# An earlier start for the first three tiles, in a kernel with an S5 scan and a gated MLP on one core

## The chip, the cores and the metric

The kernel runs on one core of one Trainium2 chip. The metric is the device time of one execution in microseconds (us). Profiles show the engines of the core: PE (matmul) and PEld (its weight loads), DVE, ACT, POOL, and SPq, the queue from which the DMAs are issued. A profile's span is 1.8 to 2.1 us shorter than the time of the same execution (261.9 us in a run of 263.81 us). The granted clock is the share of PE's full clock that the profile records (1.0 is all of it; it reads 1.00 even up to 4.4 us in the kernel before, where the warm matmuls come only every 0.43 us, so it does not show the slow start). The record calls two kernels the same when their times differ by less than 2%; all the differences below but one (e6, unclear) are of that class, and are read from ratios with their intervals, and from the traces.

## The reference, cut to what matters

```python
x = A_x                                   # 2048 x 640, bf16
xn = _layernorm(x)
z  = gelu(xn @ w_in)                      # 640 x 1728: z1 is the first half, z2 the second
z2 = _layernorm(z[..., 864:])
g  = w_sp @ z2 + b_sp                     # 2048 x 2048
mlp = (z[..., :864] * g) @ w_out
Bu = xn @ B_bar^T                         # complex; h_t = Lam_bar * h_(t-1) + Bu_t
out = x + (2 * Re(h @ C^T) + xn * Dskip) + mlp
```

## The kernel before: the parts that matter

The program is written as a list of operations with the memory that each reads and writes. A scheduler in the kernel simulates them with estimated durations and gives each engine a fixed order. PE's order is the program's; the orders of DVE, ACT and the DMA queue come out of that simulation. On the chip every engine keeps its order, whatever comes early or late.

```python
DMA_BW = 280e3                            # the simulation's DMA rate, bytes per us
...
FIRST = "x0 x1 x2 h002 h025 x3 h105 x4 x5"  # first loads: tiles of x, parts of w_in (half, from k, to k)
...
def ln_x(i):                              # statistics: bn_stats on DVE, or two sums on ACT for some tiles
    ...                                   # rstd = (var + 1e-5) ** -0.5 on POOL
    dve(... tensor_scalar(xn, x, mean, rstd, subtract, mult) ...)     # L545
def xn_T(i):                              # tiles 0-5: five PE transposes and a copy from PSUM
    if i in DMA_T:                        # tiles 6-15: one DMA transpose in SBUF      L369
...
def bu(q, tq):                            # B u: real and imaginary rows together, two PSUM banks
    for k in range(ND):
        for ri in range(2):
            r = e.matmul(ps[:, b + ri, :], btv[:, ri, k, q*128:(q+1)*128], xnTv[:, k, tq*512:(tq+1)*512], ...)
...
xn_T(0, 0); xn_T(1, 1)                    # PE's order for the first tiles
z2_half(0, 0, 2); z2_half(1, 0, 3)        # five products (k = 0..4) of one tile and one half of the z2 columns
xn_T(2, 0); z2_half(0, 1, 6); xn_T(3, 1); ...
```

After the first products (z2 of 16 tiles) PE does B u, z1, the products with w_sp ("spatial" below, 448 matmuls of 432 columns) and the output products.

Of the kernel before, what the change touches and what calls it, by code (L numbers as in the profile page):

```python
# [28 lines left out]
class _Graph:  # L29
# [6 lines left out]
    DMA_BW = 280e3  # L36
    DMA_BW_T = 215e3

    def __init__(self):
# [46 lines left out]
    def schedule(self):  # L86
# [32 lines left out]
        while left:  # L119
            best = None  # L120
            for eng, lst in avail.items():
                if not lst:
                    continue
                f = free.get(eng, 0.0)
                if eng == "pe":
                    if pei >= len(pe) or pe[pei].npred:
                        continue
                    cand = pe[pei]
                    st = max(f, cand.rdy)
                else:  # L130
                    s0 = min(max(f, o.rdy) for o in lst)
                    cand = max((o for o in lst if max(f, o.rdy) <= s0 + (self.EPS0 if s0 < self.TEPS else eps)), key=lambda o: o.tail)
                    st = max(f, cand.rdy)
                if best is None or st < best[0]:
                    best = (st, cand)
            st, op = best
            eng = op.eng
            avail[eng].remove(op)
            if eng == "pe":
                pei += 1  # L140
            op.start = st
            free[eng] = st + op.occ
            if op.nbytes:
                if op.lat > 2.2:
                    dma_free = max(st + 0.3, dma_free) + op.nbytes / self.DMA_BW_T
                    free[eng] = max(free[eng], dma_free)
                    op.done = max(st + op.occ, dma_free) + 1.7
                else:
                    dma_free = max(st + op.occ + 0.9, dma_free) + op.nbytes / self.DMA_BW
                    op.done = dma_free + op.lat - 0.9  # L150
            else:
                op.done = st + op.occ + op.lat
            order.setdefault(eng, []).append(op)
            left -= 1
            for s in op.succs:
                s.npred -= 1
                at = op.start + op.occ if eng == "pe" == s.eng else op.done
                if at > s.rdy:
                    s.rdy = at
                if s.npred == 0:  # L160
                    avail.setdefault(s.eng, []).append(s)
# [41 lines left out]
D = 640  # L203
ND = 5
# [8 lines left out]
def bass_parallel_sum__ssm_conv_s5__mixer_gmlp__prompt_kernel(  # L213
# [17 lines left out]
    with _cl.ExitStack() as _stack, nc.Block() as block:  # L231
# [106 lines left out]
        def bank(b):  # L338
            return ("ps%d" % b, 0, 1)
# [82 lines left out]

        def load_x(i, q="sp", bias=0.0):
            m = x_m[i]
            xs[i] = m
            dma(q, m.ap(D), A_x[0, i * 128:(i + 1) * 128, :], [], [m.iv()], 128 * D * 2,
                "x%d" % i, bias=bias)
# [28 lines left out]

        FIRST = "x0 x1 x2 h002 h025 x3 h105 x4 x5"
        for n, w in enumerate(FIRST.split()):
# [7 lines left out]
        for i in range(6, 11):  # L466
            load_x(i, bias=4500 - 10 * i)
        dma("sp", dk_m.ap(D), A_Dskip[:].partition_broadcast(128), [], [dk_m.iv()], 128 * 1280, "dskip")
        dma("sp", bsb_m.ap(16).rearrange("p (h j) -> p h j", h=2),
            B_b_sp.rearrange("(h r j) -> r h j", h=2, j=8), [], [bsb_m.iv()], 4096, "bsp")  # L470


        pool(lambda e: e.memset(zero_m.ap(512), 0.0), [], [zero_m.iv(0, 1024)], 0.5, "zero")
        pool(lambda e: e.memset(ident_m.ap(128), 0.0), [], [ident_m.iv()], 0.25, "id0")
# [8 lines left out]
            [zero_m.iv(1024, 16)], 1.4, "gelu table", bias=9000)  # L483
        NW = 11
        for n in range(NW):
# [18 lines left out]

        ACT_LN = (2, 5, 8, 11)
        ACT_Z2 = (8, 12)
        NHALF = 4
        BT_AT, BT_DEP = 10, 12
        LASTN = 480
        DMA_T = tuple(range(6, 16))  # L510
        xns = {}

        def ln_x(i):
# [4 lines left out]
            if i in ACT_LN:  # L518
# [5 lines left out]
                dve(lambda e: e.tensor_scalar(mean, stv[:, i, 0:1], 1.0 / D, None, op0=ALU.mult),  # L524
                    [siv(i, 0, 1)] + ([xns[1].iv()] if i == 2 else []), [mi], 0.07, "lnm%d" % i)
                dve(lambda e: e.tensor_tensor(stv[:, i, 2:3], mean, mean, ALU.mult),
# [4 lines left out]
            else:  # L531

                held = [xns[max(1, i - 2)].iv()] if 2 <= i < 4 else []
                dve(lambda e: e.bn_stats(stv[:, i, 0:6], x[:, 0:320]), [xm.iv()] + held, [siv(i, 0, 6)], 0.41, "bn%da" % i)
# [13 lines left out]
        def xn_T(i, b=None):  # L548
            xn = xns[i]
            if i in DMA_T:  # L550
# [8 lines left out]
            def tr(e):  # L559
                for u in range(ND):  # L560
                    r = e.transpose((v2 if i == 0 and u > 2 else v)[:, u, :], xn.ap(D)[:, u * 128:(u + 1) * 128], ident_m.ap(128))
                return r
            pe(tr, [xn.iv(), ident_m.iv()], [bank(b)] + ([bank(6)] if i == 0 else []), 0.3, "T%d" % i)
            if i == 0:
# [3 lines left out]
                    [xnT_m.iv(k * S * 2, 256) for k in (3, 4)], 0.21, "xnT0b")  # L568
            elif i % 2 == 0 or i == 1:
                act(lambda e: e.copy(xnTv[:, :, i * 128:(i + 1) * 128], v), [bank(b)], xnT_iv(i, i + 1),  # L570
                    ca(D, psum=True), "xnT%d" % i)
            else:
                dve(lambda e: e.tensor_copy(xnTv[:, :, i * 128:(i + 1) * 128], v), [bank(b)], xnT_iv(i, i + 1),
                    0.41, "xnT%d" % i)
# [16 lines left out]

        def z_mm(lhs, hcol, reads, name):
            b = pair()
            for k in range(ND):
                def mm(e, k=k):
                    for h in range(2):
# [6 lines left out]

        def z2_tile(i):
            b = z_mm(lambda k: xnTv[:, k, i * 128:(i + 1) * 128], 1, xnT_iv(i, i + 1), "z2_%d" % i)
            z = z2v[:, i, :]
# [6 lines left out]

        def z2_half(i, h, b):

            c = FH + h * FG
            for k in range(ND):
                pe(lambda e, k=k: e.matmul(ps[:, b, 0:FG], xnTv[:, k, i * 128:(i + 1) * 128], winv[:, k, c:c + FG],
                                           start=(k == 0), stop=(k == ND - 1)),
                   [xnT_m.iv((k * S + i * 128) * 2, 256), win_m.iv((k * 2 * FH + c) * 2, FG * 2)], [bank(b)], 0.1825, "z2_%d%d.%d" % (i, h, k))  # L620
            z = z2v[:, i, h * FG:(h + 1) * FG]
            s_ = 7 if h else 0
            act(lambda e: e.activation(z, ps[:, b, 0:FG], ACT.Gelu_apprx_tanh, accum_out=st2v[:, s_, i:i + 1]),
                [bank(b)], [z2iv(i, h), s2iv(s_, i, i + 1)], ca(FG, psum=True, acc=1), "gelu2_%d%d" % (i, h))
            if h:
# [48 lines left out]

        def bu(q, tq):

            b = pair()

            def mm(e):
                for k in range(ND):  # L680
                    for ri in range(2):
                        r = e.matmul(ps[:, b + ri, :], btv[:, ri, k, q * 128:(q + 1) * 128],  # L682
                                     xnTv[:, k, tq * 512:(tq + 1) * 512], start=(k == 0), stop=(k == ND - 1))
                return r
            pe(mm, xnT_iv(tq * 4, tq * 4 + 4) + [bt_m.iv()], [bank(b), bank(b + 1)], 2.16, "bu%d%d" % (q, tq))
            o = l_m.ap(4096, BF16, q * 8192).rearrange("p (j r t m) -> p r t j m", j=8, r=2, t=4)
            for ri in range(2):
                act(lambda e, ri=ri: e.copy(o[:, ri, tq], ps[:, b + ri, :].rearrange("p (m j) -> p j m", j=8)),  # L688
                    [bank(b + ri)], [l_m.iv((q * 8 + j) * 1024 + ri * 512 + tq * 128, 128) for j in range(8)],
                    ca(512, psum=True), "u%d%d%d" % (q, tq, ri))  # L690

# [533 lines left out]

        for i in range(5):
            ln_x(i)
        xn_T(0, 0)
        xn_T(1, 1)
        z2_half(0, 0, 2)  # L1230
        z2_half(1, 0, 3)
        xn_T(2, 0)
        z2_half(0, 1, 6)
        xn_T(3, 1)
        z2_half(1, 1, 7)
        z2_half(2, 0, 4)
        z2_half(2, 1, 5)
        xn_T(4, 0)
        z2_half(3, 0, 2)
        z2_half(3, 1, 3)  # L1240
        for i in range(4):
            load_x(i + 11)
        ln_x(5)
        xn_T(5, 1)
        ln_x(6)
        pslot[0] = 2
        for i in range(4, NT):
            if i + 3 < NT:
                ln_x(i + 3)
            z2_tile(i)  # L1250
            if i + 2 < NT:
                xn_T(i + 2)
            if i == BT_AT:
                load_bt(0, [xns[BT_DEP].iv()])
                load_bt(1, [xns[BT_DEP].iv()])
            if i == 4:
                s5_consts()
                load_x(15)
            if i == 6:
# [12 lines left out]
        for q in range(5):  # L1272
            for tq in range(4):
                bu(q, tq)
            if q < 4:
# [132 lines left out]
```

## Time and profile before

| | before |
|---|---|
| time, median | 263.57 us (263.48 to 264.02, 3 runs) |
| span of the profile | 261.9 us |
| busy share | PE 98%, DVE 93%, ACT 68% |
| first transposes of x on PE | 6.00 us |
| last z2 product ends, B u starts | 38.51, 38.80 us |

The timeline of PE of the kernel before, cut to the start (columns: start us, length us, engine, line, operation, out<-in, shapes, count, and in brackets PE's idle time before it and what ended it):

```profile
1.31 4.12 PE L486 MATMUL ps<-arena 128*128 128x512 bf16 x11 [1.31 <-POOL arena L480]
6.00 0.99 PE L561 MATMUL ps<-arena 128*128 128x128 bf16 x10 [0.57 <-DVE arena L545]
...
9.62 0.45 PE L561 MATMUL ps<-arena 128*128 128x128 bf16 x5 [0.60 <-DVE arena L545]
...
16.23 1.99 PE L597 MATMUL ps<-arena 128*128 128x432 bf16 x10
18.15 0.18 PE L800 MATMUL ps<-arena 15*128 15x15 bf16 x1
18.26 20.25 PE L597 MATMUL ps<-arena 128*128 128x432 bf16 x110
38.80 13.54 PE L682 MATMUL ps<-arena 128*128 128x512 bf16 x61 [0.29 <-DMA arena<-in_A_B_im_dram]
```

The row at 18.26 is tiles 5 to 15 without a hole, 0.184 us a matmul.

```profile
14.90 1.30 SPq L369 DMA_TRANSPOSE arena<-arena  x1
```

The DMA view of just that issue; its last number is the time in us from issue to landing:

```profile
arena<-arena SPq DMA_TRANSPOSE x1, 5.0
```

So tile 6 lands at 14.90 + 5.0 = 19.9 us, 0.2 us before PE wants it. The 1.30 us of the queue's row is not that time: it is only how long the queue was busy with the issue.

### The profile page before, as it was taken

Reading aid. Unit: us, or ns where it says so; the run is one execution under the profiler, and the core shown is the slowest. Engines: PE = TensorE matmul, PEld = TensorE weight load, DVE = VectorE, ACT = ScalarE, POOL = GpSimd, SP = SyncE. Lnnn points to the kernel's source line nnn. Section 1 sums busy time; section 2 is a strip of 40 time slices with the busy share of each in tenths; the row PEclk is TensorE's granted clock in tenths of the full one; section 3 lists DMA queues with packets and bytes.
Section 4 is the critical chain, followed back from the end, with each engine's and each line's share of the span. In section 5 each row is a group of like instructions: output and inputs, shape, how many; then the busy total and the mean of one; then the engine's idle time right before and its main releaser. Section 6 shows DMA issues by size and latency. Waiting matters only on the chain.

```text
span 261.9 us, 4305 instructions
## 1 busy us (share of the span) xinstructions
PE 255.5 (98%) x1487; PEld 151.6 (58%) x1491; DVE 242.3 (93%) x579; ACT 179.1 (68%) x323; POOL 23.0 (9%) x38
## 2 busy tenths in 40 slices
PE   6999999999999999999999999999999999999995
PEld 2555544444446777755555555555557777777773
DVE  4899997999899999999999999999999999999832
ACT  4899999989986545442333676976799889881110
POOL 4255084200000000000000000000000000000000
PEclk9999999999999999999999999999999999999999
DMA  6976899996001855496997858959562566447611
GB/s 185 361 100 131 178 198 227 293 242 123 0 0 38 222 154 163 121 274 125 270 212 161 210 123 197 172 86 270 154 209 45 136 171 154 98 130 205 169 51 50
DMA packets 88243, 41.97 MB, mean 160 GB/s; under 512 B 70975, under 2 KB 88223, under 8 KB 88223
## 3 DMA queue, kind: packets, MB, share of 16 engines
q1 hardware_dynamic: 88078, 41.66, 65.8%
q8 instruction: 11, 0.18, 0.3%
q14 instruction: 10, 0.07, 0.1%
q10 hardware_dynamic: 144, 0.05, 0.1%
HBM read 12.27 MB, written 12.45 MB: 94 GB/s over the span
## 4 chain that ended last, share of the span: by engine, by line
PE 64%; DVE 18%; ACT 7%; DMA 6%; issue 3%; SPq 1%; POOL 1%; DVEq 0%
PE ps L1146 22%; PE ps L682 16%; PE ps L999 12%; PE ps L597 11%; DVE arena L956 3%; DMA arena<-in_A_B_im_dram 2%; DMA g_scratch<-arena 2%; ACT arena L789 2%; DVE arena L734 2%; DVE arena L1039 2%; PE ps L1153 2%; DMA arena<-in_A_x_dram 2%; DVE arena L579 1%; DVE arena L921 1%; DVE arena L919 1%
## 5 line engine op out<-in xcount | busy, mean ns | idle before, releaser
L999 PE MATMUL ps<-arena 128*128 128x432 bf16 x448 | 82.1, 346 | 0.0
L999 PEld LDWEIGHTS ps<-arena 128*128 128x128 bf16 x448 | 43.7, 98 | 38.1 <-ACT arena L1012 0.4
L1146 PE MATMUL ps<-arena 128*128 128x320 bf16 x448 | 64.6, 299 | 0.1
L1146 PEld LDWEIGHTS ps<-arena 128*128 128x128 bf16 x448 | 43.5, 98 | 17.8 <-ACT ps L1175 0.5
L597 PE MATMUL ps<-arena 128*128 128x432 bf16 x280 | 51.6, 346 | 0.0
L789 ACT ACTIVATE arena<-arena 128x512 bf16<-128x512 bf16 x70 | 45.8, 712 | 4.6 <-DVE arena L793 4.5
L597 PEld LDWEIGHTS ps<-arena 128*128 128x128 bf16 x280 | 34.7, 124 | 16.1
L682 PE MATMUL ps<-arena 128*128 128x512 bf16 x196 | 43.0, 379 | 0.5 <-DMA arena<-in_A_B_im_dram 0.3
L1012 ACT ACTIVATE arena<-ps,arena 128x432 f32<-128x432 f32 (+1 forms) x32 | 19.6, 615 | 21.1 <-PE ps L999 17.0
L682 PEld LDWEIGHTS ps<-arena 128*128 128x128 bf16 x200 | 19.5, 98 | 23.9 <-DMA arena<-in_A_B_im_dram 0.5
L712 DVE SCALAR_TENSOR_TENSOR arena<-arena 128x512 f32<-128x512 bf16 x35 | 25.7, 748 | 0.4 <-ACT arena L688 0.4
L1167 DVE TENSOR_TENSOR arena<-ps,arena 128x320 bf16<-128x320 f32 (+1 forms) x40 | 18.5, 482 | 6.8 <-PE ps L1153 5.4
L688 ACT CAST arena<-ps 128x512 bf16<-128x512 f32 x40 | 21.2, 598 | 4.6 <-PE ps L682 4.5
L793 DVE TENSOR_TENSOR arena<-arena 128x1024 bf16<-128x1024 bf16 (+1 forms) x42 | 23.8, 592 | 0.0
L668 ACT ACTIVATE arena<-ps 128x864 bf16<-128x864 f32 x16 | 14.2, 890 | 13.5 <-PE ps L597 13.5
L956 DVE TENSOR_TENSOR arena<-arena 128x1024 bf16<-128x1024 bf16 x32 | 21.3, 684 | 0.5 <-DMA arena<-in_B_w_sp_dram 0.5
L734 DVE TENSOR_TENSOR arena<-arena 128x512 f32<-128x512 f32 (+2 forms) x40 | 21.4, 553 | 0.0
L717 DVE SCALAR_TENSOR_TENSOR arena<-arena 128x256 bf16<-128x256 bf16 (+1 forms) x35 | 16.7, 481 | 0.0
L714 DVE SCALAR_TENSOR_TENSOR arena<-arena 128x256 bf16<-128x256 bf16 (+1 forms) x35 | 16.7, 479 | 0.0
L1113 DVE TENSOR_TENSOR arena<-arena 128x640 bf16<-128x640 bf16 x32 | 15.2, 481 | 0.0
L1175 ACT COPY ps<-ps 128x320 f32<-128x320 f32 x16 | 6.6, 413 | 12.0 <-PE ps L1146 12.0
L1094 DVE TENSOR_TENSOR arena<-arena 128x384 bf16<-128x384 bf16 x32 | 10.9, 350 | 1.2 <-DMA arena<-g_scratch 0.9
(106 smaller groups left out, 253.9 us busy)
## 6 DMA issues: line engine op xcount, KB each, us to landing
g_scratch<-arena SPq DMA_DIRECT2D x16, 224.0 KB, 3.0
z_scratch<-arena SPq DMA_DIRECT2D x16, 216.0 KB, 2.3
arena<-z_scratch SPq DMA_DIRECT2D x8, 432.0 KB, 4.4
arena<-in_A_x_dram SPq DMA_DIRECT2D x16, 160.0 KB, 4.3
base_scratch<-arena SPq DMA_DIRECT2D x16, 160.0 KB, 2.2
arena<-base_scratch SPq DMA_DIRECT2D x16, 160.0 KB, 3.1
out_dram<-arena SPq DMA_DIRECT2D x15, 160.0 KB, 2.8
arena<-in_B_w_in_dram SPq DMA_DIRECT2D x6, 216.0 KB, 4.1
```

The source lines that it names most:

```text
L597: r = e.matmul(ps[:, b + h, 0:FG], lhs(k), winv[:, k, hcol * FH + h * FG:hcol * FH + (h + 1) * FG], start=(k == 0), stop=(k == ND - 1))
L682: r = e.matmul(ps[:, b + ri, :], btv[:, ri, k, q * 128:(q + 1) * 128], xnTv[:, k, tq * 512:(tq + 1) * 512], start=(k == 0), stop=(k == ND ...
L688: act(lambda e, ri=ri: e.copy(o[:, ri, tq], ps[:, b + ri, :].rearrange("p (m j) -> p j m", j=8)), [bank(b + ri)], [l_m.iv((q * 8 + j) * 10 ...
L712: dve(lambda e: e.scalar_tensor_tensor(tv, prev, lr, cur, op0=ALU.mult, op1=ALU.add), pr + [l_iv(q, j)] + cr, [t.iv()], cd(512) + PTR, nm ...
L734: tt = lambda o, a, b, op: (lambda e: e.tensor_tensor(o, a, b, op))
L789: act(lambda e, pv=pv, hv=hv, lo=lo, sc=sc: e.activation(pv, hv[:, lo:lo + 2, 1:257], ACT.Identity, scale=sc), [h.iv(), Civ(cn)], [m.iv((q ...
L793: dve(lambda e, mv=mv, lq=lq: e.tensor_tensor(lq, lq, mv, ALU.add), li + [m.iv(0, 1024 * n)], li, cd(512 * n, 2), "fix%s%d%d" % (nm, q0, j))
L956: dve(lambda e: e.tensor_tensor(o.ap(1024), x.ap(1024), y.ap(1024), op), [x.iv(), y.iv()], [o.iv()], cd(1024, 2), "%s_%d" % (name, j))
L999: r = e.matmul(ps[:, bk, 0:FG], lv_[:, k, :], rv[k], start=(first and k == 0), stop=(k == 7), skip_group_check=True)
L1012: act(lambda e: e.activation(o, pb(bk), ACT.Identity, bias=bias), [bank(bk)] + bi, [dst], ca(FG, psum=True, ptr=1), name)
L1146: r = e.matmul(ps[:, bk, c0:c1], lf(q), rf(q)[:, c0:c1], start=(first and q == 0), stop=(q == 7), skip_group_check=True)
L1167: dve(lambda e: e.tensor_tensor(o[0][:, c0:c1], ps[:, bk, c0:c1], y[0][:, c0:c1], ALU.add), [bank(bk), y[1]], [o[1]], cd(c1 - c0), "%s_%d" ...
```

## The change

The intent is to start PE's real work earlier. Tiles 0 to 2 are transposed as soon as their mean is subtracted. The scale 1/std commutes with the product, so it is applied in the Gelu. The true xn of these tiles is computed and transposed later, by DMA, for B u and z1. The products of the first tiles are ordered by the parts of w_in as they land. B u takes the rows of B_re first, so that B_im may come later.

```diff
+    DMA_BW0, DMA_T0 = 225e3, 9.0
-                    dma_free = max(st + op.occ + 0.9, dma_free) + op.nbytes / self.DMA_BW
+                    at = max(st + op.occ + 0.9, dma_free)
+                    dma_free = at + op.nbytes / (self.DMA_BW0 if at < self.DMA_T0 else self.DMA_BW)
 ...
-        FIRST = "x0 x1 x2 h002 h025 x3 h105 x4 x5"
+        FIRST = "x0 x1 x2 h002 h025 x3 h103 x4 h135 x5"
 ...
-        NW = 11                                  # warm matmuls on PE
+        NW = 8
-        ACT_LN = (2, 5, 8, 11)
+        ACT_LN = (5, 8, 11)
+        EARLY = (0, 1, 2)
-        BT_AT, BT_DEP = 10, 12                   # B is loaded after tile BT_DEP is normalised
+        BT_AT, BT_DEP = 10, 11
 ...
+        def ln_early(i):
+            if i < 2:
+                act(... activation(xc, xm, ACT.Copy, scale=1.0 / D, accum_out=mean) ...)
+            else:
+                early_bn(i)                      # bn_stats on DVE
+            dve(... tensor_scalar(xc, xm, mean, None, op0=ALU.subtract) ...)
+        def ln_early_std(i): ...                 # bn_stats of tiles 0 and 1, rstd
+        def ln_early_xn(i): ...                  # later: xn of tiles 0-2, and its DMA transpose
-                held = [xns[max(1, i - 2)].iv()] if 2 <= i < 4 else []
+                held = xnT_iv(2, 3) if i == 3 else [xns[i - 1].iv()] if i in HELD else []
 ...
+            act(... activation(z, ps[:, b, 0:FG], ACT.Gelu_apprx_tanh, scale=rstd if early else 1.0) ...)
 ...
         xn_T(0, 0)
         xn_T(1, 1)
-        z2_half(0, 0, 2)
-        z2_half(1, 0, 3)
+        z2_mm(0, 0, 2, 0, 2)                     # tile, half, bank, from k, to k
+        z2_mm(1, 0, 3, 0, 2)
         xn_T(2, 0)
-        z2_half(0, 1, 6) ...
+        z2_mm(0, 0, 2, 2, 5); z2_mm(1, 0, 3, 2, 5); z2_mm(2, 0, 4, 0, 5)
+        for i, b in ((0, 6), (1, 7), (2, 5)):
+            z2_mm(i, 1, b, 0, 3)
+        ...
+        load_x(14, after=[xns[LATE].iv()])       # last loads of x and Dskip after tile 3
 ...
-            for tq in range(4):
-                bu(q, tq)
+            for ri in range(2):
+                for qq in ((0, 1) if q == 0 else (q,) if q > 1 else ()):
+                    for tq in (1, 2, 3, 0):
+                        bu(qq, tq, ri)
```

The first three lines tell the simulation that DMAs are slower during the first 9 us. (Not shown: a few edits of dependencies, and a memset for the warm matmuls moved from POOL to DVE, which starts them at 1.19 instead of 1.31 us.)

More of the change, by code (lines that the diff above doesn't have):

```diff
@@ L421, in bass_parallel_sum__ssm_conv_s5__mixer_gmlp__prompt_kernel, with load_x @@
         xs = {}
-        def load_x(i, q="sp", bias=0.0):
+        def load_x(i, q="sp", bias=0.0, after=()):
             m = x_m[i]
             xs[i] = m
-            dma(q, m.ap(D), A_x[0, i * 128:(i + 1) * 128, :], [], [m.iv()], 128 * D * 2,
+            dma(q, m.ap(D), A_x[0, i * 128:(i + 1) * 128, :], list(after), [m.iv()], 128 * D * 2,
                 "x%d" % i, bias=bias)
@@ L467, in bass_parallel_sum__ssm_conv_s5__mixer_gmlp__prompt_kernel, with load_dskip @@
             load_x(i, bias=4500 - 10 * i)
-        dma("sp", dk_m.ap(D), A_Dskip[:].partition_broadcast(128), [], [dk_m.iv()], 128 * 1280, "dskip")
+        def load_dskip(after):
+            dma("sp", dk_m.ap(D), A_Dskip[:].partition_broadcast(128), after, [dk_m.iv()], 128 * 1280, "dskip")
         dma("sp", bsb_m.ap(16).rearrange("p (h j) -> p h j", h=2),
             B_b_sp.rearrange("(h r j) -> r h j", h=2, j=8), [], [bsb_m.iv()], 4096, "bsp")
-        pool(lambda e: e.memset(zero_m.ap(512), 0.0), [], [zero_m.iv(0, 1024)], 0.5, "zero")
+        dve(lambda e: e.memset(zero_m.ap(512), 0.0), [], [zero_m.iv(0, 1024)], 0.25, "zero")
         pool(lambda e: e.memset(ident_m.ap(128), 0.0), [], [ident_m.iv()], 0.25, "id0")
@@ L503, in siv @@
             return st_m.iv((i * 16 + a) * 4, (b - a) * 4)
-        ACT_LN = (2, 5, 8, 11)
+        ACT_LN = (5, 8, 11)
+        EARLY = (0, 1, 2)
+        HELD = ()
+        XNB = 0.0
+        XN_AFTER = (6, 7, 8)
         ACT_Z2 = (8, 12)
         NHALF = 4
-        BT_AT, BT_DEP = 10, 12
+        BT_AT, BT_DEP = 10, 11
         LASTN = 480
@@ L511, in bass_parallel_sum__ssm_conv_s5__mixer_gmlp__prompt_kernel, with early_bn, ln_early_std, ln_early_xn @@
         xns = {}
+        xc_m = z1o_m
+        def ln_early(i):
+            xm, xc = xs[i], xc_m[i]
+            mean, rstd = mrv[:, i, 0:1], mrv[:, i, 1:2]
+            mi, ri = mr_m.iv(i * 8, 4), mr_m.iv(i * 8 + 4, 4)
+            if i < 2:
+                act(lambda e: e.activation(xc.ap(D), xm.ap(D), ACT.Copy, scale=1.0 / D, accum_out=mean),
+                    [xm.iv()], [xc.iv(0, 1280), mi], ca(D, acc=1), "lnmean%d" % i)
+            else:
+                mean, mi = stv[:, i, 12:13], siv(i, 12, 13)
+                early_bn(i)
+            dve(lambda e: e.tensor_scalar(xc.ap(D), xm.ap(D), mean, None, op0=ALU.subtract), [xm.iv(), mi], [xc.iv(0, 1280)],
+                cd(D, 4) + PTR, "xc%d" % i)
+        def early_bn(i):
+            x, xm = xs[i].ap(D), xs[i]
+            held = [xc_m[2].iv()] if i == 1 else []
+            dve(lambda e: e.bn_stats(stv[:, i, 0:6], x[:, 0:320]), [xm.iv()] + held, [siv(i, 0, 6)], 0.41, "bn%da" % i)
+            dve(lambda e: e.bn_stats(stv[:, i, 6:12], x[:, 320:640]), [xm.iv()] + held, [siv(i, 6, 12)], 0.41, "bn%db" % i)
+            dve(lambda e: e.bn_aggr(stv[:, i, 12:14], stv[:, i, 0:12]), [siv(i, 0, 12)], [siv(i, 12, 14)], 0.13,
+                "bna%d" % i)
+        def ln_early_std(i):
+            rstd, ri = mrv[:, i, 1:2], mr_m.iv(i * 8 + 4, 4)
+            if i < 2:
+                early_bn(i)
+            dve(lambda e: e.tensor_scalar(stv[:, i, 14:15], stv[:, i, 13:14], 1e-5, None, op0=ALU.add),
+                [siv(i, 13, 14)], [siv(i, 14, 15)], 0.07, "lne%d" % i)
+            pool(lambda e: e.tensor_tensor(rstd, stv[:, i, 14:15], C("half")[:, 0:1], ALU.pow),
+                 [siv(i, 14, 15), Civ("half")], [ri], 0.5, "rstd%d" % i)
+        def ln_early_xn(i):
+            xm, xn = xs[i], xn_m[i]
+            xns[i] = xn
+            mean, mi = (mrv[:, i, 0:1], mr_m.iv(i * 8, 4)) if i < 2 else (stv[:, i, 12:13], siv(i, 12, 13))
+            dve(lambda e: e.tensor_scalar(xn.ap(D), xm.ap(D), mean, mrv[:, i, 1:2], op0=ALU.subtract, op1=ALU.mult),
+                [xm.iv(), mi, mr_m.iv(i * 8 + 4, 4), xns[XN_AFTER[i]].iv()], [xn.iv()], cd(D, 4) + 2 * PTR, "xn%d" % i)
+            dma("sp", xnTv[:, :, i * 128:(i + 1) * 128], xn.ap(D), [xn.iv()], xnT_iv(i, i + 1), 128 * D * 2, "xnT%d" % i,
+                transpose=True, bias=XNB)
         def ln_x(i):
@@ L524, in ln_x @@
                 dve(lambda e: e.tensor_scalar(mean, stv[:, i, 0:1], 1.0 / D, None, op0=ALU.mult),
-                    [siv(i, 0, 1)] + ([xns[1].iv()] if i == 2 else []), [mi], 0.07, "lnm%d" % i)
+                    [siv(i, 0, 1)], [mi], 0.07, "lnm%d" % i)
                 dve(lambda e: e.tensor_tensor(stv[:, i, 2:3], mean, mean, ALU.mult),
@@ L548, in xn_T @@
         def xn_T(i, b=None):
-            xn = xns[i]
+            xn = xc_m[i] if i in EARLY else xns[i]
             if i in DMA_T:
@@ L562, in tr @@
                 return r
-            pe(tr, [xn.iv(), ident_m.iv()], [bank(b)] + ([bank(6)] if i == 0 else []), 0.3, "T%d" % i)
+            pe(tr, [xn.iv(0, 1280), ident_m.iv()], [bank(b)] + ([bank(6)] if i == 0 else []), 0.3, "T%d" % i)
             if i == 0:
@@ L568, in xn_T @@
                     [xnT_m.iv(k * S * 2, 256) for k in (3, 4)], 0.21, "xnT0b")
-            elif i % 2 == 0 or i == 1:
+            elif (i % 2 == 0 or i == 1) and i != 2:
                 act(lambda e: e.copy(xnTv[:, :, i * 128:(i + 1) * 128], v), [bank(b)], xnT_iv(i, i + 1),
@@ L590, in s2iv, with z_mm @@
             return st2_m.iv((s_ * NT + a) * 4, (b - a) * 4)
-        def z_mm(lhs, hcol, reads, name):
+        def z_mm(lhs, hcol, reads, name, mid=None):
             b = pair()
             for k in range(ND):
+                if mid and k == 2:
+                    mid()
                 def mm(e, k=k):
@@ L602, in z_mm, with z2_tile @@
             return b
-        def z2_tile(i):
-            b = z_mm(lambda k: xnTv[:, k, i * 128:(i + 1) * 128], 1, xnT_iv(i, i + 1), "z2_%d" % i)
+        def z2_tile(i, mid=None):
+            b = z_mm(lambda k: xnTv[:, k, i * 128:(i + 1) * 128], 1, xnT_iv(i, i + 1), "z2_%d" % i, mid)
             z = z2v[:, i, :]
@@ L612, in z2_tile, with z2_mm @@
                 [z2iv(i)], [sq.iv(), s2iv(1, i, i + 1)], ca(FH, acc=1), "sq_%d" % i)
-        def z2_half(i, h, b):
-            c = FH + h * FG
-            for k in range(ND):
-                pe(lambda e, k=k: e.matmul(ps[:, b, 0:FG], xnTv[:, k, i * 128:(i + 1) * 128], winv[:, k, c:c + FG],
-                                           start=(k == 0), stop=(k == ND - 1)),
-                   [xnT_m.iv((k * S + i * 128) * 2, 256), win_m.iv((k * 2 * FH + c) * 2, FG * 2)], [bank(b)], 0.1825, "z2_%d%d.%d" % (i, h, k))
+        def z2_mm(i, h, b, k0, k1):
+            c = FH + h * FG
+            for k in range(k0, k1):
+                pe(lambda e, k=k: e.matmul(ps[:, b, 0:FG], xnTv[:, k, i * 128:(i + 1) * 128], winv[:, k, c:c + FG],
+                                           start=(k == 0), stop=(k == ND - 1), skip_group_check=True),
+                   [xnT_m.iv((k * S + i * 128) * 2, 256), win_m.iv((k * 2 * FH + c) * 2, FG * 2)], [bank(b)], 0.1825, "z2_%d%d.%d" % (i, h, k))
+            if k1 == ND:
+                z2_half(i, h, b)
+        def z2_half(i, h, b):
             z = z2v[:, i, h * FG:(h + 1) * FG]
             s_ = 7 if h else 0
-            act(lambda e: e.activation(z, ps[:, b, 0:FG], ACT.Gelu_apprx_tanh, accum_out=st2v[:, s_, i:i + 1]),
-                [bank(b)], [z2iv(i, h), s2iv(s_, i, i + 1)], ca(FG, psum=True, acc=1), "gelu2_%d%d" % (i, h))
+            early = i in EARLY
+            act(lambda e: e.activation(z, ps[:, b, 0:FG], ACT.Gelu_apprx_tanh, accum_out=st2v[:, s_, i:i + 1],
+                                       scale=mrv[:, i, 1:2] if early else 1.0),
+                [bank(b)] + ([mr_m.iv(i * 8 + 4, 4)] if early else []), [z2iv(i, h), s2iv(s_, i, i + 1)],
+                ca(FG, psum=True, acc=1, ptr=int(early)), "gelu2_%d%d" % (i, h))
             if h:
@@ L672, in z1_tile, with bu @@
             dma("sp", z1_d[n], m.ap(FH), [m.iv()], [("z1d", n, n + 1)], 128 * FH * 2, "z1st%d" % n, sem=sem)
-        def bu(q, tq):
-            b = pair()
+        nbu = [0]
+        def bu(q, tq, ri):
+            b = nbu[0] % 8
+            nbu[0] += 1
             def mm(e):
                 for k in range(ND):
-                    for ri in range(2):
-                        r = e.matmul(ps[:, b + ri, :], btv[:, ri, k, q * 128:(q + 1) * 128],
-                                     xnTv[:, k, tq * 512:(tq + 1) * 512], start=(k == 0), stop=(k == ND - 1))
+                    r = e.matmul(ps[:, b, :], btv[:, ri, k, q * 128:(q + 1) * 128],
+                                 xnTv[:, k, tq * 512:(tq + 1) * 512], start=(k == 0), stop=(k == ND - 1))
                 return r
-            pe(mm, xnT_iv(tq * 4, tq * 4 + 4) + [bt_m.iv()], [bank(b), bank(b + 1)], 2.16, "bu%d%d" % (q, tq))
+            pe(mm, xnT_iv(tq * 4, tq * 4 + 4) + [bt_m.iv(ri * 6400, 6400)], [bank(b)], 1.08, "bu%d%d%d" % (q, tq, ri))
             o = l_m.ap(4096, BF16, q * 8192).rearrange("p (j r t m) -> p r t j m", j=8, r=2, t=4)
-            for ri in range(2):
-                act(lambda e, ri=ri: e.copy(o[:, ri, tq], ps[:, b + ri, :].rearrange("p (m j) -> p j m", j=8)),
-                    [bank(b + ri)], [l_m.iv((q * 8 + j) * 1024 + ri * 512 + tq * 128, 128) for j in range(8)],
-                    ca(512, psum=True), "u%d%d%d" % (q, tq, ri))
+            act(lambda e: e.copy(o[:, ri, tq], ps[:, b, :].rearrange("p (m j) -> p j m", j=8)),
+                [bank(b)], [l_m.iv((q * 8 + j) * 1024 + ri * 512 + tq * 128, 128) for j in range(8)],
+                ca(512, psum=True), "u%d%d%d" % (q, tq, ri))
         nh = [0]
@@ L1224, in out_pair @@
                 finish()
-        for i in range(5):
-            ln_x(i)
+        EARLY_AT = (7, 8, 9)
+        LATE = 3
+        for i in EARLY:
+            ln_early(i)
+        for i in EARLY:
+            ln_early_std(i)
         xn_T(0, 0)
         xn_T(1, 1)
-        z2_half(0, 0, 2)
-        z2_half(1, 0, 3)
+        z2_mm(0, 0, 2, 0, 2)
+        z2_mm(1, 0, 3, 0, 2)
         xn_T(2, 0)
-        z2_half(0, 1, 6)
+        for i in (3, 4):
+            ln_x(i)
+        z2_mm(0, 0, 2, 2, 5)
+        z2_mm(1, 0, 3, 2, 5)
+        z2_mm(2, 0, 4, 0, 5)
+        for i, b in ((0, 6), (1, 7), (2, 5)):
+            z2_mm(i, 1, b, 0, 3)
+        z2_mm(0, 1, 6, 3, 5)
         xn_T(3, 1)
-        z2_half(1, 1, 7)
-        z2_half(2, 0, 4)
-        z2_half(2, 1, 5)
+        for i, b in ((1, 7), (2, 5)):
+            z2_mm(i, 1, b, 3, 5)
+        z2_mm(3, 0, 2, 0, 5)
         xn_T(4, 0)
-        z2_half(3, 0, 2)
-        z2_half(3, 1, 3)
-        for i in range(4):
-            load_x(i + 11)
+        z2_mm(3, 1, 3, 0, 5)
+        for i in range(11, 14):
+            load_x(i)
         ln_x(5)
-        xn_T(5, 1)
         ln_x(6)
+        load_x(14, after=[xns[LATE].iv()])
+        load_x(15, after=[xns[LATE].iv()])
+        load_dskip([xns[LATE].iv()])
         pslot[0] = 2
@@ L1249, in bass_parallel_sum__ssm_conv_s5__mixer_gmlp__prompt_kernel @@
                 ln_x(i + 3)
-            z2_tile(i)
+            z2_tile(i, (lambda: xn_T(5, 1)) if i == 4 else None)
             if i + 2 < NT:
                 xn_T(i + 2)
+            if i in EARLY_AT:
+                ln_early_xn(EARLY_AT.index(i))
             if i == BT_AT:
@@ L1257, in bass_parallel_sum__ssm_conv_s5__mixer_gmlp__prompt_kernel @@
                 s5_consts()
-                load_x(15)
             if i == 6:
```

## The prediction

> **What bounds it now.** The TensorE. By the timeline of PE, its real work starts at 6.00 us (first transposes) and runs to 258.5 us almost without a hole: 0.60 us at 9.02-9.62 (waits for DVE L545, the normalised tile 2) and 0.29 us at 38.8 (the first B u product waits for B_im). The z2 matmuls take 0.184 us each (110 in 20.25 us), so 160 need 29.5 us, the transposes about 1.7 us; z2 ends at 38.51. VectorE is nearly full too (stretches: 7.6 of 8 us from 16 to 32 us), ScalarE 8.0 of 8 from 16 to 40 us. The chain that ended last runs through DVE and ACT from 141.8 to 195.4 us; there PE waits 0.3 to 0.5 us (waits, 180-200 us: PEld L1146 on ACT L1175).
>
> **What changes.**
> 1. Start. Before, x0 lands at 3.0 us; bn_stats 2 x 0.41, aggregate, add, POOL pow 0.55 and the scaling end at 5.95. After: ACT sum of x0 (0.74 plus 0.19) ends near 3.9, DVE subtract 0.43, so T0 near 4.5: 1.5 us earlier. The scale 1/std commutes with the matmul and goes free into the Gelu.
> 2. Half-tile products may start with two parts of w_in. I estimate from bytes and the landings of x2 (4.89) and x3 (7.23), 286 GB/s, that those parts land near 5.7 and 6.8: products from 5.75 instead of 7.02; the next parts (8.2-8.4, 9.2-9.7) land before PE wants them. My walk with trace durations ends tile 3 (40 matmuls, 5 transposes) near 14.4 against 15.97: lead 1.5 us, the 0.60 hole gone with it.
> 3. Added: three subtractions (0.43), bn of tile 2 instead of ACT sums, one eviction (0.48) on DVE: about 2.5 us more DVE, about 0.7 less ACT, three more transposes on the SP queue (1.4 us each). DVE's slack is from 40 to 52 us (2.9 us, waiting for POOL and ACT), so most is absorbed.
> 4. B u by real rows: the first eight products need only B_re; B_im, now released after tile 11, lands during 8.8 us of work. The 0.29 us wait goes. Tile q=0 is complete after 12 products (13 us) instead of 8.6, but Horner started at 52.1 for another reason (Sin tables end 51.15), so I expect it near 51.
> 5. Eight warm matmuls rather than eleven. The Trainium skill (TensorE: Matmul & The Clock Gate, Part 1) gives about 3.4 us of activity before full clock; here the spacing falls from 0.43 to 0.21 us at about 4.6, after 3.3 us, which agrees. Eight end near 4.5, so the first transposes may be slow; little is lost.
>
> **Sum.** PE leads by 1.5 at 16 us and about 1.8 from the first B u product. After that PE has no holes, except at 195 us, where DVE and ACT are just in time; DVE leads by about 1, not 1.8, so I give back 0.2. Expected 263.57 - 1.6 = 262.0 us, 0.6% less. Range 261.0 to 263.3. Faster by over 2%: 0.01; within: 0.98; slower: 0.01.
>
> **What would show it.** First transposes near 4.5; no PE hole over 0.3 us from 7 to 37; last z2 matmul and first B u near 37.0, no DMA wait; z2-to-spatial border near 109.2 (was 110.95); first output products near 191 with a wait under 1 us.
>
> **What would make it wrong.** B loads queued before the transposes of tiles 12-15, starving z2; DVE too full in 8-32 us, so tiles come late; w_in parts landing later than estimated; the clock falling back with fewer warm matmuls; a lead of PE that DVE or ACT eat at the start of the output products (then about 263); the rebuilt static order opening holes later.

## More of the kernel before

The timeline of DVE around the statistics of tile 6 (bn_stats of its two halves at 11.04 and 11.91, scaling of tiles 5 and 6 at 13.92), and the DMA queue's row for the transpose of tile 6:

```profile
11.04 0.44 DVE L534 BATCH_NORM_STATS2 arena<-arena 128x6 f32<-128x320 bf16 x1
...
11.91 0.48 DVE L535 BATCH_NORM_STATS2 arena<-arena 128x6 f32<-128x320 bf16 x1
...
13.92 0.95 DVE L545 TENSOR_SCALAR arena<-arena 128x640 bf16<-128x640 bf16 x2
```

## The result, and the profile after

The changed kernel took 263.71 us (263.47 to 263.89, 4 runs) against 263.79 us (263.48 to 264.36, 4 runs) for the kernel before (three of them the runs above). A ratio here is the mean time of one kernel's runs over that of the other's of the same rounds, so it is not quite the ratio of the medians. It was 0.9994 with a 95% interval of 0.9972 to 1.0015: no gain that these runs show, and outside the range of 261.0 to 263.3.

The timeline of PE of the changed kernel, the same stretch (L611 are the transposes, L670 and L649 z2 products, L743 B u):

```profile
1.19 3.59 PE L490 MATMUL ps<-arena 128*128 128x512 bf16 x8 [1.19 <-DVE arena L477]
4.57 0.74 PE L611 MATMUL ps<-arena 128*128 128x128 bf16 x5
5.58 0.68 PE L611 MATMUL ps<-arena 128*128 128x128 bf16 x5 [0.27 <-DVE arena L534]
6.09 0.53 PE L670 MATMUL ps<-arena 128*128 128x432 bf16 x2
7.04 0.54 PE L670 MATMUL ps<-arena 128*128 128x432 bf16 x2 [0.42 <-ACT arena L620]
...
17.21 2.00 PE L649 MATMUL ps<-arena 128*128 128x432 bf16 x10
20.62 18.42 PE L649 MATMUL ps<-arena 128*128 128x432 bf16 x100 [1.41 <-DMA arena<-arena]
38.88 43.33 PE L743 MATMUL ps<-arena 128*128 128x512 bf16 x200
```

The early start is there: transposes at 4.57 instead of 6.00, and tile 5's products at 17.21 instead of 18.26, so PE leads by 1.05 us. Then PE waits 1.41 us for a DMA out of SBUF, which is the transpose of tile 6, and tile 6 starts at 20.62 against 18.26 + 10 x 0.184 = 20.10 before. The lead has become a lag of 0.52 us. The 0.29 us wait for B_im is gone, and B u starts 0.08 us later than before. Tile 6's way through DVE and the DMA queue in the changed kernel:

```profile
12.19 0.49 DVE L623 COPY arena<-ps 128x640 bf16<-128x640 bf16 x1 [0.36 <-PE ps L611]
...
13.02 0.48 DVE L584 BATCH_NORM_STATS2 arena<-arena 128x6 f32<-128x320 bf16 x1
...
13.48 0.48 DVE L585 BATCH_NORM_STATS2 arena<-arena 128x6 f32<-128x320 bf16 x1
...
15.10 0.95 DVE L595 TENSOR_SCALAR arena<-arena 128x640 bf16<-128x640 bf16 x2
```

```profile
16.08 1.30 SPq L371 DMA_TRANSPOSE arena<-arena  x1
```

The DMA view for that issue, and below it for the load of x6, issued at 6.69:

```profile
arena<-arena SPq DMA_TRANSPOSE x1, 4.5
```

```profile
arena<-in_A_x_dram SPq DMA_DIRECT2D x1, 160.0 KB, 4.1
```

x6 is in SBUF at 6.69 + 4.1 = 10.8 us, as before (6.29 + 4.6 = 10.9). But its statistics start at 13.02, not 11.04. Between these times DVE stands idle for 0.36 us ahead of 12.19, waiting for PE, with tile 6's data at hand. The Trainium skill (TensorE: Matmul & The Clock Gate, Part 1) says that ACT and DVE are strict FIFO; this idle time of 0.36 us beside ready work agrees.

The simulation in the changed kernel, printed after the prediction, puts the landing of x6 at 12.09 us and the statistics of tile 6 at 12.70. That of the kernel before says 10.41 and 10.57. The new slower rate is why. (The same print-out gives a total of 260.83 us before and 260.72 after: by the scheduler's own account the change gains 0.1 us.) The same print-out of later runs gives 259.48 for e1, 262.11 for e7 and 263.38 for e6: the measured times come in this order too. (It gives 261.56 for e5, which was not borne out.)

### The profile page after: what moved, and what is told of

It reads as the page before. It is cut to its first block, busy times and chain, and to the rows that moved or that the text cites. A ratio compares the mean times of both kernels' runs of the same rounds, so it can differ in the third digit from the quotient of the medians. Undisturbed runs are those within 1.5% of the kernel's fastest.

```text
span 262.1 us, 4316 instructions
## 1 busy us (share of the span) xinstructions
PE 255.7 (98%) x1488; PEld 151.4 (58%) x1488; DVE 244.6 (93%) x584; ACT 178.8 (68%) x322; POOL 22.6 (9%) x37
## 4 chain that ended last, share of the span: by engine, by line
PE 65%; DVE 20%; DMA 8%; issue 4%; ACT 1%; POOL 0%; SPq 0%; DVEq 0%
PE ps L1206 23%; PE ps L649 18%; PE ps L743 16%; DVE arena L1016 5%; PE ps L1059 4%; DMA g_scratch<-arena 4%; DVE arena L794 2%; PE ps L670 2%; DMA arena<-arena 2%; PE ps L1213 2%; DVE arena L1132 1%; DMA arena<-in_B_w_sp_dram 1%; DVE arena L853 1%; DVE arena L1079 1%; DVE arena L772 1%
## 5 line engine op out<-in xcount | busy, mean ns | idle before, releaser
L649 PE MATMUL ps<-arena 128*128 128x432 bf16 x280 | 51.9, 346 | 1.4 <-DMA arena<-arena 1.4
L649 PEld LDWEIGHTS ps<-arena 128*128 128x128 bf16 x280 | 34.5, 124 | 17.9 <-DMA arena<-arena 1.8
L743 PE MATMUL ps<-arena 128*128 128x512 bf16 x200 | 43.3, 379 | 0.0
L743 PEld LDWEIGHTS ps<-arena 128*128 128x128 bf16 x200 | 19.6, 98 | 23.5
L772 DVE SCALAR_TENSOR_TENSOR arena<-arena 128x512 f32<-128x512 bf16 x35 | 25.5, 742 | 0.1
L748 ACT CAST arena<-ps 128x512 bf16<-128x512 f32 x40 | 22.2, 610 | 3.0 <-PE ps L743 3.0
L663 ACT ACTIVATE arena<-arena 128x864 bf16<-128x864 bf16 x12 | 11.2, 934 | 0.0
```

What stands on the lines that cost most here:

```text
L649: r = e.matmul(ps[:, b + h, 0:FG], lhs(k), winv[:, k, hcol * FH + h * FG:hcol * FH + (h + 1) * FG], start=(k == 0), stop=(k == ND - 1))
L743: r = e.matmul(ps[:, b, :], btv[:, ri, k, q * 128:(q + 1) * 128], xnTv[:, k, tq * 512:(tq + 1) * 512], start=(k == 0), stop=(k == ND - 1))
L748: act(lambda e: e.copy(o[:, ri, tq], ps[:, b, :].rearrange("p (m j) -> p j m", j=8)), [bank(b)], [l_m.iv((q * 8 + j) * 1024 + ri * 512 + t ...
L772: dve(lambda e: e.scalar_tensor_tensor(tv, prev, lr, cur, op0=ALU.mult, op1=ALU.add), pr + [l_iv(q, j)] + cr, [t.iv()], cd(512) + PTR, nm ...
```

## The experiments

Three theories: (A) the order on DVE, from the pessimistic DMA rate, makes tile 6 late; (B) DVE is simply too full after the change; (C) the first DMA transpose is slow because it is the first. All eleven runs gave correct results.

### e1: only the DMA rate of the simulation set back

```diff
-    DMA_BW0, DMA_T0 = 225e3, 9.0
+    DMA_BW0, DMA_T0 = 280e3, 9.0
```

> One number of the change undone: the slower DMA rate in the schedule's own model (225 for the first 9 us) set back to 280, which changes only the static orders: tile 6's bn_stats come two places earlier on DVE. Theory A (order): in the changed kernel x6 lands at 10.8 but its bn_stats start at 13.0, because the model believed in 12.1, so xn6 is 1.2 us later than before and its transpose lands 1.4 us after PE wants it. A expects the transpose of tile 6 issued near 14.9 and landed near 19.5, the PE wait of 1.41 us down to 0.4 or less, and the time 1.0 to 1.4 us below the changed kernel (ratio to before near 0.996). Theory B (DVE too full: 2.5 us of added work) expects tile 6 still issued after 15.7 and the time within 0.3 us of the changed kernel. Theory C (slow first transpose) expects a gain only as far as the issue moves.

Measured: 262.13 us against 263.64 before, ratio 0.9951 (0.9927 to 0.9974). Lines of e1: DVE's two statistics of tile 6, the scaling of tiles 5 and 6, the issue of the transpose, its landing, and PE:

```profile
11.39 0.48 DVE L584 BATCH_NORM_STATS2 arena<-arena 128x6 f32<-128x320 bf16 x1
...
12.79 0.48 DVE L585 BATCH_NORM_STATS2 arena<-arena 128x6 f32<-128x320 bf16 x1
...
14.47 0.95 DVE L595 TENSOR_SCALAR arena<-arena 128x640 bf16<-128x640 bf16 x2
```

```profile
15.45 1.31 SPq L371 DMA_TRANSPOSE arena<-arena  x1
```

```profile
arena<-arena SPq DMA_TRANSPOSE x1, 3.5
```

```profile
17.34 20.25 PE L649 MATMUL ps<-arena 128*128 128x432 bf16 x110
37.64 3.62 PE L743 MATMUL ps<-arena 128*128 128x512 bf16 x16
```

The hole is gone and B u starts at 37.64, 1.24 us earlier than in the changed kernel. The work on DVE is the same, so B falls as the whole cause. (The one number changes the place of many operations in the orders of DVE, ACT and the DMA queue, not of tile 6's statistics alone; that the gain comes from tile 6 is read from the trace.) But the gain at tile 6 has two parts. The transpose was issued 0.63 us earlier, half of the 1.2 us expected, and it landed in 3.5 us instead of 4.5. With 4.5 us it would have landed at 19.95, 0.8 us after PE's want at 17.34 + 1.84 = 19.18: an estimate from these lines. The order is not the sole difference from the kernel before: the issue is still 0.55 us later than its 14.90, with 2.3 us more busy time on DVE in the page of the changed kernel (244.6 against 242.3 us).

### e2 and e3: is it tile 6, and is the first transpose slow because it is the first?

```diff
 # e2: tile 6 by PE
-        DMA_T = tuple(range(6, 16))
+        DMA_T = tuple(range(7, 16))
 # e3: one more DMA transpose, ahead of tile 6's; engine orders unchanged
+        dma("sp", xnTv[:, :, 1920:2048], xns[LATE].ap(D), [xns[LATE].iv()], xnT_iv(15, 16), 1, "warmT", transpose=True, bias=-1000.0)
```

> The changed kernel with tile 6 transposed on PE (0.28 us there and an eviction) instead of by DMA; tiles 7 and on by DMA. If the wait belongs to the DMA round trip of the first transpose, whoever it is, tile 7 becomes the first and lands 4.5 to 5 us after its issue at about 17.6, near 22.3, with PE wanting it near 21.2: the wait moves to tile 7 and shrinks to about 1 us; time within 0.5 us of the changed kernel. If it was only tile 6 that was late, the wait goes and the time falls by about 1.1 us.

> The changed kernel with one more DMA transpose, of tile 3 into the place of tile 15 (overwritten later), queued at about 12.3 us, before the transpose of tile 6; the orders of PE, DVE and ACT are the same as in the changed kernel. Theory C: the first transpose is slow because it is the first (4.5 us to landing here, 5.0 before, later ones 2.6 to 3.6), so tile 6's will land about 3 us after its issue at 16.1, near 19.1 to 19.4, the PE wait shrinks to 0 to 0.3 us and the time falls by about 1.1 us. If the 4.5 us has another cause (what else the queues carry at 16 to 20 us), tile 6 still lands near 20.6 and the time stays within 0.3 us of the changed kernel.

Measured: e2 263.14 us, ratio 0.9988 (0.9967 to 1.0008); e3 263.37 us, 0.9990 (0.9971 to 1.0008). PE's waits in the two, first e2, then e3:

```profile
23.78 14.78 PE L649 MATMUL ps<-arena 128*128 128x432 bf16 x80 [0.95 <-DMA arena<-arena]
```

```profile
20.30 18.42 PE L649 MATMUL ps<-arena 128*128 128x432 bf16 x100 [1.17 <-DMA arena<-arena]
```

In e2 the wait moved on, as expected, but to tile 8 and not to tile 7: the 30 products of tiles 5 to 7 ran through. The first transpose there, issued at 17.70, landed in only 2.7 us, not 4.5 to 5. In e3 the added transpose went out at 12.69, and tile 6's, now the second, still took 4.3 us (issued 16.00). Both contradict C.

The kept traces show what goes with a slow transpose. The instruction rows of the DMA view (queue, kind, packets, MB, share of the 16 DMA engines) from issue to landing of tile 6's transpose, first in the changed kernel (16.08 to 20.57), then in e1 (15.45 to 18.97):

```profile
q8 instruction: 1, 0.02, 1.2%
q14 instruction: 1, 0.01, 0.5%
```

```profile
q8 instruction: 1, 0.02, 1.7%
```

Each is a fetch of the program's instructions, of 16 and of 8 KB. Two began while the transpose was under way in the changed kernel (at 17.23 and 19.08), one in e1 (16.38; the next came at 19.20, after the landing), none during e2's first transpose. Over all 13 traces, tile 6's transpose took 3.2 to 3.7 us with one fetch (five traces) and 4.3 to 5.0 us with two (seven). Of the 102 transposes within SBUF with no fetch between issue and landing, 99 took 2.56 to 2.71 us; with one fetch, 22 of 47 took over 2.8 us. So the later issue seems to have cost twice: it also kept the transpose in flight until the second fetch. This goes together in the traces; no run moves a fetch alone, so it is not shown as the cause.

By itself, taking tile 6 off the DMA does not help while the tiles behind it are as late.

### e4 and e5: parts of the change put into the kernel before

e4 is the kernel before with only the new B u. e5 is the kernel before with only the slow DMA rate in its simulation.

> The kernel before with one part of the change alone: the B u products by real rows first, one bank each. Expected: the 0.29 us wait for B_im at 38.8 goes, PE starts B u near 38.5 and runs on; time 0.2 to 0.4 us below before (ratio 0.9985 to 0.9992). A rival, that the DVE and ACT chain before the output products eats any lead of PE, expects no change of time and a wait at about 195 us that grows by 0.3 us.

> The mirror of e1: the kernel before with nothing but the slower DMA rate (225 for the first 9 us) in the schedule's model. Theory A: the static DVE order then puts tile 6's statistics later although x6 lands at 10.9 as ever; its transpose is issued about 1 us later than 14.9, near 15.7 to 16.3, lands near 20.5 to 21 against a want of 20.1, PE waits 0.4 to 1.0 us more, and the time is 0.3 to 1.0 us above before. If the order does not matter: same time within 0.3 us.

Measured: e4 263.50 us, ratio 0.9997 (0.9971 to 1.0023); e5 263.79 us, 0.9994 (0.9971 to 1.0017). In e4's trace B u starts without a wait, at 38.91. But the run's warm matmuls took 4.88 us instead of 4.12 and the first z2 products started at 7.29 instead of 7.02; later PE waited 0.65 us for ACT at 168.98. The 0.29 us is inside the noise, and e4 decides nothing about time.

e5 missed its expectation. The transpose of tile 6 was issued 0.51 us later (15.41) but landed in 4.5 us, so at 19.9, just ahead of PE's want at 18.14 + 1.84 = 19.98. PE then waited 0.85 us for B_im. The kernel before survives the bad order, and the changed kernel, whose PE asks 0.9 us earlier (19.05, from 17.21 + 1.84) and whose transpose is issued 0.67 us later, does not. So the slow rate alone does not make the hole.

### e6 and e7: what the other parts are worth, on top of e1

e6 is e1 with the old `bu`, called for `tq in range(4)`. e7 is e1 with PE's old order of the first products:

```diff
-        z2_mm(0, 0, 2, 0, 2)
-        z2_mm(1, 0, 3, 0, 2)
+        z2_mm(0, 0, 2, 0, 5)
+        z2_mm(1, 0, 3, 0, 5)
         xn_T(2, 0)
+        z2_mm(0, 1, 6, 0, 5)
+        xn_T(3, 1)
 ...
```

> e1 with the B u part undone (both rows of a tile together, tile group 0 first, as in the kernel before). The prediction counted this part as 0.29 us. But the real rows of tiles 0 to 2 are now transposed a second time, late, and B_im is issued near 33: the old order asks first for tile group 0 and for both B. Expected: PE waits 2 to 4 us at 37.6 for a DMA and the time is 2 to 4 us above e1, 1 to 2.5 above before. If the part is worth only the 0.29 us: within 0.5 us of e1.

> e1 with the products of the first tiles in the old order on PE (each half-tile's five parts in one go, before the next tile), w_in still in parts. Expected: PE waits for the second part of w_in (lands 6.9) and for tile 3, start of tile 4 about 1 to 2 us later than e1's 15.0, most of the lead lost: time 0.8 to 1.8 us above e1, near before. If the earlier start alone makes the lead: within 0.4 us of e1.

Measured: e6 268.20 us, ratio 1.0172 (1.0140 to 1.0204); e7 265.62 us, 1.0059 (1.0026 to 1.0091). PE's hole in e6, then in e7:

```profile
41.33 8.89 PE L741 MATMUL ps<-arena 128*128 128x512 bf16 x34 [3.84 <-DMA arena<-arena]
```

```profile
12.38 0.45 PE L611 MATMUL ps<-arena 128*128 128x128 bf16 x5 [2.54 <-DVE arena L595]
```

The new B u order is not a gain of 0.29 us, as the prediction booked it. It is what makes the early start possible. The old order asks first for tiles 0 to 3, whose true xn is now transposed last (queued at 35.99 in e6), and PE waits 3.84 us. In the same way the new order of products is needed because tile 3 is not ready when the old order asks for it.

At the median both lost more than their holes, and in their traces the clock fell after the hole. The stretches of e7, 1 us each (columns: stretch, its length, busy time of PE, PEld, DVE, ACT, POOL with counts, then the granted clock, DMA share and GB/s):

```profile
12.00:13.00 1.00, 0.62 (x7) 0.49 (x8) 1.00 (x5) 1.00 (x3) 0.36 (x1) 1.00 0.71 191
...
14.00:15.00 1.00, 1.00 (x4) 0.46 (x3) 1.00 (x5) 0.21 (x2) 0.28 (x2) 0.50 0.67 228
```

After a hole of 2.54 us the granted clock was about 0.50 from 13 until about 16.5 us, and the 15 products from 12.67 took 4.58 us, against 2.90 for 15 products in the kernel before. Three of the six runs of e7 had a mean clock of 0.994 and took 266.26 to 267.36 us; the three at 1.0 took 264.55 to 264.98, which is 2.4 to 2.9 us above e1, about the hole alone. All six of e6 were at 0.994 or 0.987.

### e8: eleven warm matmuls instead of eight, on top of e1

> e1 with eleven warm matmuls on PE instead of eight. They end near 5.3 instead of 4.7, so the first transposes start about 0.7 us later; the second tile's (5.67) hardly move, and T0's five are faster at full clock (0.45 instead of 0.74). Expected: time 0.1 to 0.6 us above e1. If the clock fell back with eight, as the prediction feared, eleven would be faster than e1 by some 0.3 us.

Measured: 263.46 us, ratio 0.9984 (0.9957 to 1.0011). The first line is the warm matmuls, the second the transposes of tiles 0 and 1:

```profile
1.19 4.87 PE L490 MATMUL ps<-arena 128*128 128x512 bf16 x11 [1.19 <-DVE arena L477]
5.85 1.27 PE L611 MATMUL ps<-arena 128*128 128x128 bf16 x10
```

The three warm matmuls cost more than expected. In this trace all eleven ran slowly, tile 0's transposes started 1.28 us later than in e1, and tile 5's products 1.1 us later (18.45 against 17.34). Eight did better here, though against e1 of other rounds, and eleven do not always run slowly (4.12 us in the trace of the kernel before). The clock did not fall back with eight: in e1's trace 22 products from 7.82 took 4.18 us, 0.19 us each.

### e9, e10, e11: the changed kernel and e1 again on one chip, and one step more

e11 is e1 with tile 1's copy out of PSUM shared between ACT and DVE, as tile 0's already is.

```diff
+            if i == 1:
+                act(lambda e: e.copy(xnTv[:, 0:3, 128:256], v[:, 0:3]), ...)
+                dve(lambda e: e.tensor_copy(xnTv[:, 3:5, 128:256], v2[:, 3:5]), ...)   # v2: another bank
```

> The changed kernel itself once more, beside e10 on one chip, because the trace of e1 shows two things at once: the transpose of tile 6 issued 0.63 us earlier (15.45 against 16.08) and landing in 3.5 us instead of 4.5. Expected: ratio to before 0.998 to 1.001; the PE wait for tile 6's transpose is there again, 1.0 to 1.6 us; issue to landing again over 4 us if it belongs to the kernel, anything from 2.7 to 5 if it is chance.

> e1 once more. Theory A expects the ratio to before 0.993 to 0.997 and to the changed kernel of the same rounds about 0.995, tile 6's transpose issued near 15.4 and PE waiting at most 0.4 us for it. If e1 was luck with a DMA landing: ratio to the changed kernel 0.998 or more, and a wait of about 1 us in this trace.

> e1 with the eviction of tile 1's transposes shared by ACT (three fifths) and DVE (two fifths, from another PSUM bank), as tile 0's is. In e1 PE waits 0.41 us for ACT's 0.69 us copy at 6.8 to 7.2. Expected: the second pair of products 0.2 to 0.3 us earlier, all later starts as much earlier unless tile 6's transpose now comes late; time 0 to 0.3 us below e10, within the noise of these rounds.

Measured, against 263.70 us before: e9 263.09 us, ratio 0.9965 (0.9934 to 0.9995); e10 262.53 us, 0.9946 (0.9914 to 0.9977); e11 262.40 us, 0.9943 (0.9905 to 0.9981). One of the runs before took 266.47 us and pulls all three ratios down: without it they are 0.9975, 0.9957 and 0.9949. So in these rounds the changed kernel itself was a little faster than the kernel before, and its median lies inside the predicted range. PE's wait in e9:

```profile
20.46 18.43 PE L649 MATMUL ps<-arena 128*128 128x432 bf16 x100 [1.37 <-DMA arena<-arena]
```

The wait of the changed kernel is there again, with 4.5 us to landing again. In e10 and e11 there is none, with an issue near 15.1 and 3.5 us to landing again. The landing times repeat in each kernel's second trace, and so do the fetches: two while the transpose was under way in e9, one in e10.

What the removed wait is worth in time is less sure. The mean of e10 is 262.59 us and that of e9 263.08, so 0.998 and not the 0.995 that A expected. Over the rounds of e1, the ratio to before was 0.9951 against the changed kernel's 0.9994 in its own rounds. Starts on PE, in us:

| | before | after | e9 | e1 | e10 | e11 |
|---|---|---|---|---|---|---|
| z2 of tile 5 | 18.26 | 17.21 | 17.10 | 17.34 | 17.06 | 16.98 |
| B u | 38.80 | 38.88 | 38.94 | 37.64 | 37.36 | 37.28 |
| spatial products | 110.95 | 111.24 | 111.09 | 109.79 | 109.51 | 109.43 |
| output products | 192.90 | 193.27 | 192.85 | 191.55 | 191.76 | 191.19 |
| last products | 258.24 | 258.71 | 257.89 | 256.58 | 256.89 | 256.30 |

e10 leads e9 by 1.58 us at B u and at the spatial products, and by 1.00 at the end. The waits view of e10 from 110 to 200 us shows PE's weight loads waiting for ACT's copies out of PSUM:

```profile
PEld ps L1059 <- ACT arena L1072: 0.7, 2, 0.5
PEld ps L1059 <- ACT ps L1081: 0.5, 1, 0.5
...
PEld ps L1206 <- ACT ps L1235: 0.3, 1, 0.3
```

e9 has no such row there. But the changed kernel's trace has the first of these rows too (0.8 us), with no lead to lose, and e1 and e11, which lead by about as much, take 81.76 us from the first spatial to the first output product, as e9 does (e10: 82.25). So the rows do not show that a lead is lost in the spatial stage, and why e10 kept less of its lead stays open. The first Horner step of the scan (one step of h_t = Lam_bar * h_(t-1) + Bu_t; L712 before, L772 after) began at 52.14 us before, at 55.23 in the changed kernel and at 54.93 in e1, so DVE has 3 us less in hand although PE is not behind. No run here tests whether that costs time.

e1, e10 and e11 were faster than the kernel before by about 0.5%, with intervals clear of 1; against the changed kernel of the same rounds, e10 and e11 were faster by 0.2 to 0.3% by the means. e11's further gain over e10 is within the noise, though its trace shows what was expected of it: the second pair of products at 6.60 instead of 6.89.

## Why the prediction was wrong, point by point

- **Bound by PE, early start near 4.5, w_in in time: right.** The first transposes came at 4.57. The parts of w_in landed at 5.4, 6.9, 8.4 and 9.5 (issue plus landing), against 5.7, 6.8, 8.2 to 8.4 and 9.2 to 9.7.
- **"Lead 1.5 us": mis-sized.** It measured 1.05 us at tile 5. Tile 0's transposes took 0.74 us, and two waits of 0.27 and 0.42 us for DVE and ACT are not named in the prediction.
- **"Three more transposes on the SP queue (1.4 us each)", "most is absorbed", "no PE hole over 0.3 us from 7 to 37": the step that failed.** It names DMA transposes only as 1.4 us of the queue for each of the three added ones. It does not weigh tile 6's, which takes 5.0 us to landing in the profile before and had 0.2 us in hand. A PE that starts a microsecond earlier needs its next supplier a microsecond earlier. In the changed kernel that supplier was 1.18 us later (issue 16.08 against 14.90), and a hole of 1.41 us took the lead. Its list of risks has DVE too full from 8 to 32 us, and last, nearer to what happened, "the rebuilt static order opening holes later". e1 and e10 show that the orders that follow from one number in the scheduler's model were enough to open or close the hole, in part by an earlier issue and in part by a shorter time to landing.
- **Three lines of the diff were not read for what they do.** The prediction does not mention the model's DMA rate. Setting it back removed the hole (e1, e10).
- **B u, "the 0.29 us wait goes": right but mis-valued.** The wait went. Without this part e1 loses about 6 us (e6: 268.20 against 262.13, on another chip), in part through the clock, so it pays for the early start rather than adding to it.
- **Horner "near 51": wrong.** It began at 55.23.
- **Eight warm matmuls, "little is lost": right, and more.** Eleven cost 0.9 us by the ratios and 1.3 by the medians (e8 against e1, in different rounds).
- **"I give back 0.2" late: not contradicted.** Over the kernel before, e10 leads by 1.44 us at B u and by 1.35 at the last products, and e1 by 1.16 and 1.66. Against e9, e10 gives back about 0.6 us.

Without the hole (e1, e10) the kernel takes 262.1 to 262.5 us, close to the 262.0 that was predicted. The predicted sum left out one wait of 1.41 us, nearly as large as the 1.6 us forecast. In time its removal brought 0.5 us in the same rounds (e9 to e10) and 1.6 us across rounds (the changed kernel to e1), so the wait's share in the missing gain is known only within these bounds.

## What to carry to other kernels

Before starting an engine earlier, take its next few suppliers and work out, from issue to landing, by how much each is ahead of its consumer: a margin of 0.2 us means that the gain ends there unless the supplier moves too. Where orders are fixed by a simulation in the kernel, a number in its model is as much a change as an operation is, its printed total is worth reading before the prediction (it gained only 0.1 us here), and an in-order engine will hold ready work behind work that the model believed would be ready first. Some parts of a change carry no gain themselves but pay for another part; undoing them singly, as e6 and e7 did, shows which.

## What the Trainium skill lacked or had wrong

- TensorE: Matmul & The Clock Gate, "HAM oscillation" gives as the rule no PE idle gaps over about 3.4 us. In e7 a hole of 2.54 us was followed by a granted clock of 0.50, and three of six runs showed a lowered mean clock (0.994). On the other side, the holes of 1.41 us (after) and 1.17 us (e3) left the clock at 1.00.
- The same page, Part 1, says that the number of cold matmuls varies between runs. The eight warm matmuls took 3.26 us (e9) to 3.60 us (e1), and the eleven 4.12 us (before) to 4.88 us (e4). What it lacks is that the warm-up matmuls themselves can be the bound of the start: eleven instead of eight moved the first transposes from 4.57 (e1) to 5.85 us (e8).
- DMA: Bandwidth & Descriptors, "DMA Transpose (X-bar)" names no time from issue to landing for one transpose within SBUF. Here one of 128 x 640 elements took 2.56 to 2.71 us in 99 of the 102 cases with no instruction fetch meanwhile, and 3.2 to 5.0 us for tile 6's with one or two, while the queue was busy for 1.3 us.
- No page gives what an instruction fetch costs a DMA transpose in flight (nearest is Runtime: NRT & Kernel Launch, "Instruction fetch mechanics"). In these traces tile 6's transpose took 0.6 to 1.0 us more with one fetch, and 1.6 to 2.3 us more with two, than the 2.6 to 2.7 us of transposes without.
